# A fixed instruction order to the attention's end, and slot sums of several batches in TensorE column groups

## The chip, the core and the metric

One core of one Trainium2 chip runs the whole program. The metric is device microseconds of one execution, as the median of several runs. Engines are named as in the profile: PE (TensorE), ACT (ScalarE), DVE (VectorE), POOL (GpSimd), SP (SyncE, which issues nearly all DMAs).

## The reference, cut to what matters

Attention with a learned position bias, then a soft mixture of experts over all tokens, then a top-1 mixture.

```python
# attention: B, H, S, D = 4, 8, 576, 64
scores = q @ k.T / sqrt(D) + bias[h]            # bias: a small MLP of relative positions, 32 hidden
attn   = softmax(scores)                        # exp(s - max), divided by its sum
x      = attn @ v                               # -> [B*S, H*D] = [2304, 512]
# soft MoE: 8 experts, 4 slots each (32 slots), F = 1024
logits     = x @ phi                            # [2304, 32]
d          = exp(logits - logits.max(0)); d /= d.sum(0) + 1e-9      # over ALL 2304 tokens
slot_input = d.T @ x                            # [32, 512]: the slot sums
slot_out   = relu(slot_input[e] @ w1[e]) @ w2[e]                    # per expert, 4 slots each
c          = softmax(logits, over slots);  x = c @ slot_out
# then: skip gate, argmax expert, one dense expert per token, added to x
```

## The kernel before, in words

**Bias.** The position bias of all heads is built first by 36 calls of bias_batch and written to a DRAM scratch. The list order says in which sequence, and load_bias brings a head pair's rows back, 128 queries (t = 0 to 3; the last 64 of two heads are t = 4) at a time.

**Attention.** The work is 16 pairs n (head pair hp = n // 4, batch b = n % 4). ops_of(n) returns named steps of one pair. A name ends in p for the PE part and e for the evacuation: KG0p/KG0e, QG0p/QG0e, LASTp/LASTe are transposes of k and q and their copies; SW0, SW1, SW8 swap halves of k on POOL; QKtjp is the score product of query tile t, head j (line 412), QKtje its bias add with running minimum on DVE (line 429), EXtj the exponential on ACT (line 435). For t = 0 to 2, HIt (POOL, line 440) and LOt (DVE, line 444) split the result into two fp16 halves and TDt (line 449) is a transposing DMA issued on SP; for t = 3 and 4 PE transposes (T3ap to T3cp, T4ap, T4bp). AVtj are the products with v (lines 503 to 523), N0 and N1 the division into xnat (lines 544 to 556), XTp/XTe and XUp/XUe transposes of the result, LG0 and LG1 the logits of a pair's channels (lines 605 and 614), summed over hp in lgT. TD, LK, LQ, LV, BA, BM are SP's DMAs; BA of the last head pair loads expert weights (weight_piece) in place of bias.

**The order.** SCHED gives every step a number; todo sorts all steps of all pairs by n * II + number. Only the order counts, not the number's size. From the first score product up to 15 * II + first the steps are inside manual_schedule: each engine and SP run them exactly in that order. What lies behind that point (the last pair's later steps, the slot sums), the bias build and all that follows the attention are placed by the framework's planner, by its own cost estimate.

**Slot sums.** When the last head pair has its logits, for each batch: SA (slot_exp: maximum, negation, exponential with sum), SB (slot_T: five 32-wide transposes and a copy to dn), SC (slot_in: five fp32 products over token tiles, 32 output rows by 512 columns, lines 254 and 257, and two copies into sis). The four batches have different maxima, kept in nm; after the attention a matmul of nm with sel (line 744), a chain of small DVE/ACT steps (fx, fs, fz, lines 749 to 757) makes a factor for each batch and slot, and a product of sis with fsel (line 761) adds the four batches up. The result goes to sT, the stationary operand of the first expert product ph (line 773).

**Weights.** Both expert matrices are 64 pieces of 512 KB (weight_piece), i = 0 to 31 for w1 (line 773) and 32 to 63 for w2 (line 854). They rotate through 25 buffers: pieces 0 to 2 by BA; 3 to 12 in buffers of q, k and bias that are free late in the attention (NW + 10 = 13); 13 to 24 in twelve tiles x0 to x11 that lie where the attention's pools were. From piece 25 on, a piece is issued when the product that read its buffer is done. All go through SP's queue.

Of the kernel before, what the change touches and what calls it, by code (L numbers as in the profile page):

```python
# [59 lines left out]
def soft_moe_attention_kernel(ctx, tc, q, k, v, w1, b1, w2, phi, mw1, mw2,  # L60
# [168 lines left out]
    def slot_exp(b):  # L229
# [8 lines left out]
        act.activation(dT[r, 0:S], lgT[r, 0:S], AF.Exp, bias=nm[r, b:b + 1], scale=1.0, accum_out=nm[r, 4 + b:5 + b])  # L238

    def slot_T(b):  # L240

        r = slice(b * 32, (b + 1) * 32)
        pt = ps_t.tile([P, 512], F32, name="pt")
        dT = sl[0]
        for c in range(5):
            o = c * P if c < 4 or b % 2 == 0 else S - P
            pe.transpose(pt[:, c * NSL:(c + 1) * NSL], dT[r, o:o + P], ident[r, r])
        vec.tensor_copy(dn[:, b], pt[:, 0:5 * NSL])

# [1004 lines left out]
```

## Time and profile before

| | |
|---|---|
| median of 3 runs | 524.05 us (522.62 to 531.67) |
| profiled execution, its own time | 519.99 us |
| span from first to last instruction | 518.1 us |
| mean granted PE clock, share of 2.4 GHz | 0.942 |
| PE busy, of the span | 89% |
| DVE, ACT, POOL busy | 66%, 57%, 48% |
| last attention product ends | 346.6 us |
| first expert product begins | 391.7 us |
| last weights landed, second expert product ends | 450.6 us, 453.0 us |

The profiled execution is one run; times in the rows are microseconds from its first instruction. Its own time lies 4.06 us under the median of the timed runs, so a change in the span is carried over to the median as a difference.

### The profile page before, as it was taken

What the parts mean: (1) busy time and instruction counts of PE and PEld (TensorE: products, weight loads), DVE (VectorE), ACT (ScalarE), POOL (GpSimd) and SP (SyncE); (2) the same over time, 40 slices, a digit from 0 to 9 for tenths busy, and PEclk for the clock granted to TensorE, in tenths of its full rate; (3) what the DMA queues carried; (4) which work ended last, traced back from release to release, by engine and by line L of the source; (5) the groups of instructions that cost most, each with busy time, mean ns of one, the idle gap of its engine ahead of it and who ended that gap; (6) DMA issues with size and microseconds to landing.
All of it is one profiled execution on the core that took longest, in us unless ns stands there. A gap on an engine that the chain in (4) does not pass through costs nothing.

```text
span 518.1 us, 12026 instructions
## 1 busy us (share of the span) xinstructions
PE 460.6 (89%) x4539; PEld 347.0 (67%) x4539; DVE 344.0 (66%) x842; ACT 293.0 (57%) x565; POOL 247.2 (48%) x291
## 2 busy tenths in 40 slices
PE   4999989999999999999999999789759549769993
PEld 2566668999999899999999998662115224155472
DVE  6999966888887887778878786821231390046564
ACT  4889877877787787777887777411110021016610
POOL 5600049999889799797997994400020000001000
PEclk9999997999999999999999999988887958968999
DMA  6677658999999999999999999999003999845056
GB/s 175 222 258 259 213 198 189 219 206 224 198 229 192 220 216 220 214 211 210 185 203 211 231 221 214 269 320 373 1 1 120 394 387 387 296 143 183 22 173 202
DMA packets 154080, 111.53 MB, mean 215 GB/s; under 512 B 120257, under 2 KB 126913, under 8 KB 154017
## 3 DMA queue, kind: packets, MB, share of 16 engines
q1 hardware_dynamic: 152112, 107.47, 81.9%
q10 hardware_dynamic: 1824, 2.97, 1.7%
q8 instruction: 38, 0.62, 0.5%
q0 software_dynamic: 80, 0.26, 0.2%
q14 instruction: 26, 0.20, 0.1%
HBM read 66.97 MB, written 15.34 MB: 159 GB/s over the span
## 4 chain that ended last, share of the span: by engine, by line
PE 73%; DMA 11%; DVE 9%; issue 2%; POOL 2%; ACT 1%; SPq 0%; ACTq 0%; DVEq 0%; POOLq 0%
PE sc L412 14%; PE sc L155 10%; PE av L523 6%; PE av L507 5%; PE av L512 4%; DMA bias<-in_moe_w_dram 4%; PE pt L254 4%; PE pt L369 4%; PE pt L478 3%; DMA eT<-ehl 3%; PE pt L605 2%; DMA x<-in_moe_w_dram 2%; PE sc L418 2%; PE av L519 2%; PE ph L773 1%
## 5 line engine op out<-in xcount | busy, mean ns | idle before, releaser
L429 DVE CUSTOM_DVE_ANT_0 e<-sc,bias 128x576 f32<-128x576 f32 x128 | 95.2, 754 | 22.8 <-PE sc L412 22.4
L412 PE MATMUL sc<-k,qT 128*128 128x288 f32 x512 | 98.8, 321 | 1.7 <-POOL k L382 1.0
L435 ACT ACTIVATE e<-e,st 128x576 f32<-128x576 f32 x128 | 93.9, 771 | 5.2 <-DVE st L429 4.7
L440 POOL TENSOR_SCALAR ehl<-e 128x1152 f16<-128x1152 f32 x48 | 64.9, 1354 | 57.7 <-ACT e L435 56.0
L382 POOL TENSOR_SCALAR k<-k 64x512 fp32r<-64x512 f32 (+1 forms) x96 | 78.8, 821 | 20.5 <-ACT k L376 10.3
L412 PEld LDWEIGHTS sc<-k,qT 128*128 128x128 f32 x512 | 74.6, 195 | 7.5 <-DVE xnat L556 2.3
L444 DVE SCALAR_TENSOR_TENSOR ehl<-e,ehl 128x1152 f16<-128x1152 f32 x48 | 77.6, 1618 | 1.5 <-POOL ehl L440 1.5
L155 PE MATMUL sc<-hid,w2b 128*32 128x288 f32 x576 | 57.2, 420 | 3.0 <-DVE hid L151 3.0
L151 DVE TENSOR_SCALAR hid<-ll,nib 128x576 f32<-128x576 f32 x117 | 58.1, 574 | 0.0
L523 PE MATMUL av<-v,eT 128*128 128x65 f16 x1152 | 51.5, 194 | 0.0
L155 PEld LDWEIGHTS sc<-hid,w2b 128*32 128x32 f32 x576 | 32.3, 110 | 24.8 <-DVE hid L151 4.7
L523 PEld LDWEIGHTS <-eT 128*128 128x128 f16 x1152 | 44.4, 98 | 4.3 <-issue 3.3
L484 ACT ACTIVATE eTf<-pt 128x512 f32<-128x512 f32 (+1 forms) x48 | 23.5, 489 | 27.3 <-PE pt L478 27.2
L158 ACT ACTIVATE ev<-sc,offs,ipi 128x576 f32<-128x576 f32 x36 | 29.8, 828 | 10.4 <-PE sc L155 9.9
L981 POOL TENSOR_SCALAR Lt<-rk 128x128 f16<-128x128 f32 x1 | 0.3, 298 | 73.4 <-PE pbig L854 73.4
L507 PE MATMUL av<-tv,eTf 128*128 128x128 f32 x256 | 35.3, 280 | 0.0
L507 PEld LDWEIGHTS av<-tv,eTf 128*128 128x128 f32 x256 | 32.0, 191 | 0.0
L376 ACT ACTIVATE qT<-pt 128x512 fp32r<-128x512 f32 x32 | 19.1, 596 | 14.0 <-PE pt L369 13.8
L478 PE MATMUL pt<-ident,e 128*128 128x128 f32 x144 | 24.6, 282 | 0.9 <-ACT eTm L469 0.9
L327 POOL TENSOR_TENSOR sq<-tq,sq 128x576 fp32r<-128x576 f32 x16 | 23.1, 1441 | 1.3
L544 DVE TENSOR_SCALAR rs<-av 128x2 f32<-128x2 f32 (+1 forms) x64 | 8.0, 156 | 23.6 <-PE av L507 23.0
L327 POOL TENSOR_TENSOR sk<-tk,sk 128x576 fp32r<-128x576 f32 x16 | 23.0, 1435 | 1.3
(322 smaller groups left out, 871.6 us busy)
## 6 DMA issues: line engine op xcount, KB each, us to landing
x<-in_moe_w_dram SPq DMA_DIRECT2D x30, 512.0 KB, 10.6
scratch<-ev SPq DMA_DIRECT2D x36, 288.0 KB, 4.1
bias<-scratch SPq DMA_DIRECT2D x16, 576.0 KB, 4.9
tn<-in_v_dram SPq DMA_DIRECT2D x32, 224.0 KB, 4.9
bias<-in_moe_w_dram SPq DMA_DIRECT2D x13, 512.0 KB, 10.8
k<-in_moe_w_dram SPq DMA_DIRECT2D x12, 512.0 KB, 7.6
tk<-in_k_dram SPq DMA_DIRECT2D x16, 288.0 KB, 5.3
tq<-in_q_dram SPq DMA_DIRECT2D x16, 288.0 KB, 3.6
```

Source lines behind the costliest of these rows:

```text
L151: vec.tensor_scalar(out=hid, in0=src, scalar1=nib[:, gi:gi + 1], scalar2=None, op0=ALU.max)
L155: pe.matmul(pb[c * 32:(c + 1) * 32, hh, 0:288], lhsT=w2b, rhs=hid[:, hh * 288:(hh + 1) * 288], start=True, stop=True)
L327: pool.tensor_tensor(out=z[name][:, :, 1, :], in0=t, in1=z[name][:, :, 0, :], op=ALU.subtract)
L382: pool.tensor_scalar(out=k1[64 * i:64 * i + 64, :, u], in0=k0[64 - 64 * i:128 - 64 * i, :, u], scalar1=1.0, scalar2=1.0, op0=ALU.mult, op1 ...
L412: pe.matmul(sc[:, hh, 0:288], lhsT=l_, rhs=kf[i][:, o:o + 288], start=(i == 0), stop=(i == 1))
L429: vec.tensor_tensor_reduce(out=z["e", t][:, o].rearrange("p (a j) -> p a j", a=2), in0=z.pop(("sc", t, j))[:, :, 0:288], in1=bias_t[hp, t] ...
L435: act.activation(ee, ee, AF.Exp, bias=z["m", t][:, j:j + 1], scale=-1.0)
L440: pool.tensor_scalar(out=eh[:, 0], in0=z["e", t], scalar1=ES, scalar2=1.0, op0=ALU.mult, op1=ALU.mult)
L444: vec.scalar_tensor_tensor(out=eh[:, 1], in0=z.pop(("e", t)), scalar=ES, in1=eh[:, 0], op0=ALU.mult, op1=ALU.subtract)
L478: pe.transpose(pt[:, c], z["e", 3][:, (4 * g + c) * P:(4 * g + c + 1) * P], ident)
L507: pe.matmul(av[:, oj:oj + P], lhsT=eT[:, 5 * j + c], rhs=w, start=False, stop=j == 1 and c == 3)
L523: pe.matmul(av[:, oj:oj + VD], lhsT=eT[:, ei, 5 * j + c], rhs=v16[:, vi, c, j], start=False, stop=lastt and j == 1 and k_ == 2 and c == 3)
```

## The change: what it does

SCHED gets new numbers. The last four pairs (n = 12 to 15) get numbers of their own from a table LAST, one per pair, and manual_schedule now holds from the first score product to the last slot step. The bias batches are built in another sequence, with query tile t = 2 first. The weight pieces 3 to 12 are all issued behind the last transposing DMA of pair 15.

The slot steps become separate: SAm (maximum), SAx (exponential), SBp, SBe (transposes, copy), SC0 to SC4 (token tile c of batches 0, 1 and 2, each batch in its own group of 32 columns, into one PSUM tile), SCe and SCd (copies). Batch 3 is summed by S3p: its token tiles 0 to 3 go to the four column groups and tile 4 to group 0 again; the four partial rows stay apart in sis3, a borrowed e buffer, and are added up by the product FSp, which now has two operands (sl[1] and sis3) and so twice the matmuls. FX holds the factor chain of before, with four more copies on ACT for batch 3's factors; its tiles move to the const pool.

```diff
 II = 14100
-SCHED = {"LK": 0, "LQ": 607, "LV": 13878, "BA": 24197, "TD0": 34151, "TD1": 42871, "TD2": 32292, "KHI": 4505,
...
-         "LG0p": 64050, "LG0e": 65023, "LG1p": 73289, "LG1e": 73968}
+SCHED = {"LK": 0, "LQ": 2593, "LV": 9168, "BA": 20815, "BM": 30422, "TD0": 32207, "TD1": 41463, "TD2": 29378,
...
+         "EX31": 30379, "QK40p": 23432, "QK40e": 25178, "EX40": 26731, "HI0": 24394, "LO0": 26955, "AV00": 43025,
+         "AV01": 43844, "HI1": 30962, "LO1": 36034, "AV10": 43513, "AV11": 45277, "HI2": 23540, "LO2": 24437,
+         "AV20": 31523, "AV21": 33272, "T3ap": 30786, "T3ae": 31293, "T3bp": 32041, "T3be": 33438, "T3cp": 33299,
...
+         "XUp": 48366, "XUe": 49339, "LG0p": 56034, "LG0e": 56061, "LG1p": 57644, "LG1e": 58386}
+LAST = {"LK": [-1201, -2566, -6806, 1324], "LQ": [-3383, -757, -6246, 7269], "LV": [16548, 16126, 21689, 34057],
+         "BA": [25594, 164680, 55239, 158463], "TD0": [35809, 49689, 53834, 128993],
+         "TD1": [49729, 57859, 94140, 180561], "TD2": [35969, 41139, 51880, 83599], "KHI": [3363, -299, -219, 4361],
...
+         "QK11p": [21994, 21949, 43799, 92252], "QK11e": [22394, 27941, 51840, 108240],
...
+         "LG1e": [27941, 166501, 213593, 299837], "SAm0": [313897, 180561, 243397, 370297],
+         "SAx0": [160837, 205052, 257577, 376364], "SBp0": [418704, 271637, 290100, 382907],
+         "SBe0": [29484, 304160, 304160, 384437], "SAm1": 171293, "SAx1": 186623, "SBp1": 271597, "SBe1": 279301,
+         "SC0": 313937, "SC1": 325351, "SC2": 342097, "SC3": 397007, "SC4": 411147, "SCe": 481607, "SCd": 481727,
+         "FXp": 384397, "FX": 397047, "S3p": 404644, "S3e": 411107, "S3d": 481687, "FSp": 747365, "FSe": 767415}
...
+    fx = const.tile([NSL, 4], F32, name="fx")
+    fs = const.tile([NSL, 4], F32, name="fs")
+    fz = const.tile([NSL, 2], F32, name="fz")
+    fsel = const.tile([P, 2, NSL], F32, name="fsel")
+    fsx = const.tile([P, P], F32, name="fsx")
...
-    def slot_exp(b):
+    def slot_max(b):
...
-        dT = sl[0]
+            pool.memset(sl[1][96:P], 0.0)
         vec.tensor_reduce(out=nm[r, b:b + 1], in_=lgT[r, 0:S], axis=AX.X, op=ALU.max)
         vec.tensor_scalar(out=nm[r, b:b + 1], in0=nm[r, b:b + 1], scalar1=-1.0, scalar2=None, op0=ALU.mult)
-        act.activation(dT[r, 0:S], lgT[r, 0:S], AF.Exp, bias=nm[r, b:b + 1], scale=1.0, accum_out=nm[r, 4 + b:5 + b])
+
+    def slot_exp(b):
+        act.activation(sl[0][r, 0:S], lgT[r, 0:S], AF.Exp, bias=nm[r, b:b + 1], scale=1.0, accum_out=nm[r, 4 + b:5 + b])
...
     def slot_T(b):
-
         r = slice(b * 32, (b + 1) * 32)
-        pt = ps_t.tile([P, 512], F32, name="pt")
-        dT = sl[0]
+        pt = sl_pt[b] = ps_t.tile([P, 512], F32, name="pt")
         for c in range(5):
             o = c * P if c < 4 or b % 2 == 0 else S - P
-            pe.transpose(pt[:, c * NSL:(c + 1) * NSL], dT[r, o:o + P], ident[r, r])
-        vec.tensor_copy(dn[:, b], pt[:, 0:5 * NSL])
-
-    def slot_in(b):
-        r = slice(b * 32, (b + 1) * 32)
-        pt = ps_t.tile([P, 512], F32, name="pt")
-        for c in range(4):
-            pe.matmul(pt[r], lhsT=dn[:, b, c * NSL:(c + 1) * NSL], rhs=X[0][:, 4 * b + c, :], start=(c == 0), stop=False)
-        sis = sl[1]
-        u = slice((b % 2) * 64, (b % 2) * 64 + 64)
-        pe.matmul(pt[r], lhsT=dn[u, b, 4 * NSL:], rhs=X[0][u, 16 + b // 2, :], start=False, stop=True)
-        act.copy(sis[r, 0:256], pt[r, 0:256])
-        vec.tensor_copy(sis[r, 256:512], pt[r, 256:512])
+            pe.transpose(pt[:, c * NSL:(c + 1) * NSL], sl[0][r, o:o + P], ident[r, r])
+
+    def slot_dn(b):
+        vec.tensor_copy(dn[:, b], sl_pt.pop(b)[:, 0:5 * NSL])
+
+    def slot_sum(b, c, dst, start, stop):
+        u = slice((b % 2) * 64, (b % 2) * 64 + 64) if c == 4 else slice(0, P)
+        pe.matmul(dst, lhsT=dn[u, b, c * NSL:(c + 1) * NSL], rhs=X[0][u, 4 * b + c if c < 4 else 16 + b // 2, :], start=start, stop=stop)
+
+    sl_pt = {}
 
...
         if hp == 3 and b:
             for i, bb in enumerate(bs):
-                for x, f in (("SA", slot_exp), ("SB", slot_T), ("SC", slot_in)):
+                for x, f in (("SAm", slot_max), ("SAx", slot_exp), ("SBp", slot_T), ("SBe", slot_dn)):
                     ops[f"{x}{i}"] = lambda f=f, bb=bb: f(bb)
+        if n < NP - 1:
+            return ops
+
+        def sc(c):
+            if c == 0:
+                z["sl"] = ps_s.tile([P, 2, 512], F32, name="sc")
+            for bb in range(3):
+                slot_sum(bb, c, z["sl"][bb * 32:(bb + 1) * 32, 0], c == 0, c == 4)
+
+        each([f"SC{c}" for c in range(5)], sc)
+
+        @part
+        def SCe():
+            act.copy(sl[1][0:96, 0:256], z["sl"][0:96, 0, 0:256])
+
+        @part
+        def SCd():
+            vec.tensor_copy(sl[1][0:96, 256:512], z["sl"][0:96, 0, 256:512])
+
+        @part
+        def FXp():
+            z["pf"] = ps_t.tile([P, 512], F32, name="pt")
+            pe.matmul(z["pf"][0:NSL, 0:8], lhsT=sel[:, 0:NSL], rhs=nm, start=True, stop=True)
+
+        @part
+        def FX():
+            pf = z["pf"]
+            vec.tensor_reduce(out=fz[:, 0:1], in_=pf[0:NSL, 0:4], axis=AX.X, op=ALU.min)
+            act.activation(fx, pf[0:NSL, 0:4], AF.Exp, bias=fz[:, 0:1], scale=-1.0)
+            vec.tensor_tensor(out=fs, in0=fx, in1=pf[0:NSL, 4:8], op=ALU.mult)
+            vec.tensor_reduce(out=fz[:, 1:2], in_=fs, axis=AX.X, op=ALU.add)
+            vec.tensor_scalar(out=fz[:, 1:2], in0=fz[:, 1:2], scalar1=1e-9, scalar2=None, op0=ALU.add)
+            vec.reciprocal(out=fz[:, 1:2], in_=fz[:, 1:2])
+            vec.tensor_scalar(out=fx, in0=fx, scalar1=fz[:, 1:2], scalar2=None, op0=ALU.mult)
+            for g in range(4):
+                act.activation(fsel[g * 32:(g + 1) * 32, 1], sel[0:NSL, 0:NSL], AF.Copy, scale=fx[:, 3:4])
+                if g < 3:
+                    vec.tensor_scalar(out=fsel[g * 32:(g + 1) * 32, 0], in0=sel[0:NSL, 0:NSL], scalar1=fx[:, g:g + 1],
+                                      scalar2=None, op0=ALU.mult)
+
+        @part
+        def S3p():
+            z["s3"] = ps_s.tile([P, 2, 512], F32, name="sc")
+            for c in range(5):
+                g = c % 4 * 32
+                slot_sum(3, c, z["s3"][g:g + 32, 0], c < 4, c in (1, 2, 3, 4))
+            z["sis3"] = e_p.tile([P, 2 * S], F32, name="e")[:, 0:512]
+
+        @part
+        def S3e():
+            act.copy(z["sis3"][:, 0:256], z["s3"][:, 0, 0:256])
+
+        @part
+        def S3d():
+            vec.tensor_copy(z["sis3"][:, 256:512], z["s3"][:, 0, 256:512])
+
+        @part
+        def FSp():
+            z["pfs"] = ps_t.tile([P, 512], F32, name="pt")
+            for kc in range(4):
+                for i, x in enumerate((sl[1], z["sis3"])):
+                    pe.matmul(z["pfs"][:, kc * NSL:(kc + 1) * NSL], lhsT=x[:, kc * P:(kc + 1) * P], rhs=fsel[:, i],
+                              start=i == 0, stop=i == 1)
+
+        @part
+        def FSe():
+            vec.tensor_copy(fsx, z["pfs"][:, 0:P])
+
...
-    for i, x in enumerate(("SA0", "SA1", "SB0", "SB1", "SC0", "SC1")):
-        SC[x] = SC["LG1e"] + 1000 + 500 * i
-    SC["BM"] = 35452
-    todo = sorted((n * II + SC[x], n, x) for n in range(NP) for x in OPS[n])
+    SC["BM"] = 30422
+
+    def place(n, x):
+        if n < NP - 4:
+            return SC[x]
+        return LAST[x][n - NP + 4] if type(LAST[x]) is list else LAST[x]
+
+    todo = sorted((n * II + place(n, x), n, x) for n in range(NP) for x in OPS[n])
...
-    order = [*range(8), *range(16, 24), *range(8, 16), *range(32, 36), *range(24, 32)]
+    order = [*range(16, 24), *range(16), *range(24, 36)]
...
-    msc = None
-    for t_, n, x in todo:
-        on = first + 0 <= t_ < 15 * II + first + 0
-        if on and not msc and 'PE Pool Activation DVE SP':
-            msc = ExitStack()
-            msc.enter_context(tc.manual_schedule(engines={getattr(mybir.EngineType, x) for x in 'PE Pool Activation DVE SP'.split()}))
-        elif not on and msc:
-            msc.close()
-            msc = None
-        if True:
+    with tc.manual_schedule(engines=fixed):
+        last_td = max(place(NP - 1, f"TD{t}") for t in range(3)) + (NP - 1) * II
+        for t_, n, x in todo:
             OPS[n][x]()
-            if n == NP - 1 and x in {'TD0': 1, 'TD1': 1, 'TD2': 2}:
-                for _ in range({'TD0': 1, 'TD1': 1, 'TD2': 2}[x]):
+            if t_ == last_td:
+                while len(wq) < NW + 10:
                     weight_piece()
-    if msc:
-        msc.close()
-    while len(wq) < NW + 10:
-        weight_piece()
...
-        pf = p1.tile([P, 10], F32, name="pw")
-        pe.matmul(pf[0:NSL, 0:8], lhsT=sel[:, 0:NSL], rhs=nm, start=True, stop=True)
...
-        for b in range(4):
-            vec.tensor_scalar(out=fsel[b * 32:(b + 1) * 32], in0=sel[0:NSL, 0:NSL], scalar1=fx[:, b:b + 1],
-                              scalar2=None, op0=ALU.mult)
-        pt = ps.tile([P, 512], F32, name="pc")
-        for kc in range(4):
-            pe.matmul(pt[:, kc * NSL:(kc + 1) * NSL], lhsT=sis[:, kc * P:(kc + 1) * P], rhs=fsel, start=True, stop=True)
-
...
-            pt[:, 0:P].rearrange("p (k e i) -> p e k i", k=4, e=E))
+            fsx.rearrange("p (k e i) -> p e k i", k=4, e=E))
```

Sorted by their numbers, PE's last steps after the change are: QK11p.15 T4bp.15 T3ap.15 AV20.15 T3bp.15 AV40.15 XUp.14 AV41.15 AV21.15 LG1p.13 XTp.14 AV30.15 T3cp.15 LG0p.14 AV31.15 AV00.15 LG1p.14 AV10.15 AV01.15 AV11.15 XUp.15 SBp1.13 SBp0.13 XTp.15 SBp0.14 LG0p.15 LG1p.15 SC0 SC1 SC2 SBp0.15 FXp SC3 S3p SC4 FSp (the number behind the point is the pair). SP's last are: TD2.14 TD0.14 BA.14 TD1.14 TD2.15 TD0.15 BA.13 BA.15 TD1.15, then pieces 3 to 12.

## Rows read from the trace of the kernel before

**Rows 1.** Windows, of three pair periods: length, each engine's busy time, granted clock, DMA share, GB/s

```profile
69.75:86.56 16.81, 14.03 (x84) 12.40 (x83) 11.65 (x28) 13.47 (x26) 13.89 (x15) 0.80 0.75 181
...
288.35:305.16 16.81, 16.81 (x202) 15.55 (x202) 13.12 (x36) 14.13 (x29) 16.00 (x17) 1.00 1.12 227
...
321.98:338.79 16.81, 13.98 (x156) 11.69 (x154) 11.13 (x28) 7.83 (x15) 5.68 (x25) 0.98 1.08 270
```

**Rows 2.** Chain that ended last, 346 to 392 us: start, length, what

```profile
346.27 0.32 PE av L507 x2
...
350.66 0.42 DVE xnat L556
...
351.93 5.23 PE pt L254 x8
357.16 0.97 PE pt L257 x2
358.14 3.55 PE pt L254 x8
...
363.56 0.66 PE pt L581 x4
...
379.58 5.10 PE pt L254 x8
...
386.54 0.16 DVE fz L749
...
389.16 1.66 PE pc L761 x8
...
391.73 6.92 PE ph L773 x85
```

**Rows 3.** Windows, of the stretches around the slot sums

```profile
365.00:392.00 27.00, 17.61 (x52) 5.95 (x56) 6.93 (x23) 2.95 (x8) 3.22 (x3) 0.83 0.02 1
```

**Rows 4.** Chain that ended last, 408 to 453 us: the two expert products

```profile
408.65 0.64 PE ph L773 x8
...
427.36 2.14 PE pbig L854 x8
...
439.84 10.71 DMA x<-in_moe_w_dram
450.59 2.36 PE pbig L854 x8
```

**Rows 5.** Windows, while the weights stream and from logits to transposed exponentials

```profile
374.40:379.60 5.20, 1.81 (x11) 0.63 (x10) 2.58 (x6) 1.47 (x4) 3.22 (x3) 0.96 0.00 0
...
440.00:450.00 10.00, 7.93 (x32) 1.01 (x28) 0.00 (x0) 0.00 (x0) 0.00 (x0) 1.00 1.03 381
```

**Rows 6.** Timeline of SP, DMA issues around the attention's end

```profile
322.51 3.77 SPq L186 DMA_DIRECT2D bias<-in_moe_w_dram  x3
...
327.72 12.47 SPq L449 DMA_TRANSPOSE eT<-ehl  x3
```

**Rows 7.** Chain that ended last, 254 to 272.5 us: first and last of 49 pieces

```profile
253.95 0.13 PE sc L418
...
272.13 0.44 PE pt L478 x4
```

**Rows 8.** Page, groups by line: busy us, mean ns of one, idle before

```profile
L429 DVE CUSTOM_DVE_ANT_0 e<-sc,bias 128x576 f32<-128x576 f32 x128 | 95.2, 754 | 22.8 <-PE sc L412 22.4
...
L435 ACT ACTIVATE e<-e,st 128x576 f32<-128x576 f32 x128 | 93.9, 771 | 5.2 <-DVE st L429 4.7
L440 POOL TENSOR_SCALAR ehl<-e 128x1152 f16<-128x1152 f32 x48 | 64.9, 1354 | 57.7 <-ACT e L435 56.0
...
L444 DVE SCALAR_TENSOR_TENSOR ehl<-e,ehl 128x1152 f16<-128x1152 f32 x48 | 77.6, 1618 | 1.5 <-POOL ehl L440 1.5
```

**Rows 9.** Tile ehl, 200 to 340 us: its transposes from issue to landing

```profile
DMA to landing us min/median/max: 4.6/6.6/8.9
```

**Rows 10.** Timeline of PE, one product over four column groups

```profile
479.20 1.07 PE L1082 MATMUL y<-w2e,hO 128*32 128x512 f32 x8
```

More of the change, by code (lines that the diff above doesn't have):

```diff
@@ L35 @@
 II = 14100
-SCHED = {"LK": 0, "LQ": 607, "LV": 13878, "BA": 24197, "TD0": 34151, "TD1": 42871, "TD2": 32292, "KHI": 4505,
[12 rows of a table removed]
+SCHED = {"LK": 0, "LQ": 2593, "LV": 9168, "BA": 20815, "BM": 30422, "TD0": 32207, "TD1": 41463, "TD2": 29378,
+         "KHI": 5296, "KLO": 7286, "QHI": 7955, "QLO": 8985, "VA": 16708, "VH": 23835, "VLO": 29151, "KG0p": 8978,
[11 rows of a table added]
+LAST = {"LK": [-1201, -2566, -6806, 1324], "LQ": [-3383, -757, -6246, 7269], "LV": [16548, 16126, 21689, 34057],
+         "BA": [25594, 164680, 55239, 158463], "TD0": [35809, 49689, 53834, 128993],
+         "TD1": [49729, 57859, 94140, 180561], "TD2": [35969, 41139, 51880, 83599], "KHI": [3363, -299, -219, 4361],
+         "KLO": [6397, 1171, 4429, 7389], "QHI": [4641, 6462, 7409, 15359], "QLO": [5278, 6502, 7729, 15439],
[35 rows of a table added]
+         "XTe": [96094, 111599, 152361, 283051], "XUp": [332440, 78392, 134552, 213593],
[7 rows of a table added]
 ETB = 4
@@ L65, in soft_moe_attention_kernel @@
     const = ctx.enter_context(tc.tile_pool(name="const", bufs=1))
+    fixed = {getattr(mybir.EngineType, x) for x in ('PE', 'Activation', 'DVE', 'Pool', 'SP')}
     dpool = ctx.enter_context(tc.tile_pool(name="dpool", bufs=1, space=DRAM))
@@ L74, in soft_moe_attention_kernel @@
     identr = const.tile([P, P], F32R, name="identr")
+    fx = const.tile([NSL, 4], F32, name="fx")
[3 more added lines that the diff above has]
+    fsx = const.tile([P, P], F32, name="fsx")
     scratch = dpool.tile([S, H, S], F32, name="scratch")
     pool.memset(nm, 0.0)
+    pool.memset(fsel, 0.0)
     kctx = ctx.enter_context(ExitStack())
@@ L237, in slot_exp @@
         vec.tensor_scalar(out=nm[r, b:b + 1], in0=nm[r, b:b + 1], scalar1=-1.0, scalar2=None, op0=ALU.mult)
-        act.activation(dT[r, 0:S], lgT[r, 0:S], AF.Exp, bias=nm[r, b:b + 1], scale=1.0, accum_out=nm[r, 4 + b:5 + b])
+    def slot_exp(b):
+        r = slice(b * 32, (b + 1) * 32)
+        act.activation(sl[0][r, 0:S], lgT[r, 0:S], AF.Exp, bias=nm[r, b:b + 1], scale=1.0, accum_out=nm[r, 4 + b:5 + b])
     def slot_T(b):
         r = slice(b * 32, (b + 1) * 32)
-        pt = ps_t.tile([P, 512], F32, name="pt")
-        dT = sl[0]
+        pt = sl_pt[b] = ps_t.tile([P, 512], F32, name="pt")
         for c in range(5):
             o = c * P if c < 4 or b % 2 == 0 else S - P
-            pe.transpose(pt[:, c * NSL:(c + 1) * NSL], dT[r, o:o + P], ident[r, r])
-        vec.tensor_copy(dn[:, b], pt[:, 0:5 * NSL])
-    def slot_in(b):
-        r = slice(b * 32, (b + 1) * 32)
-        pt = ps_t.tile([P, 512], F32, name="pt")
-        for c in range(4):
-            pe.matmul(pt[r], lhsT=dn[:, b, c * NSL:(c + 1) * NSL], rhs=X[0][:, 4 * b + c, :], start=(c == 0), stop=False)
-        sis = sl[1]
-        u = slice((b % 2) * 64, (b % 2) * 64 + 64)
-        pe.matmul(pt[r], lhsT=dn[u, b, 4 * NSL:], rhs=X[0][u, 16 + b // 2, :], start=False, stop=True)
-        act.copy(sis[r, 0:256], pt[r, 0:256])
-        vec.tensor_copy(sis[r, 256:512], pt[r, 256:512])
+            pe.transpose(pt[:, c * NSL:(c + 1) * NSL], sl[0][r, o:o + P], ident[r, r])
[5 more added lines that the diff above has]
+    sl_pt = {}
     def ops_of(n):
@@ L741, in soft_moe_attention_kernel @@
         pool.memset(hT, 0.0)
-        pf = p1.tile([P, 10], F32, name="pw")
-        pe.matmul(pf[0:NSL, 0:8], lhsT=sel[:, 0:NSL], rhs=nm, start=True, stop=True)
-        fx = sp.tile([NSL, 4], F32, name="fx")
-        fs = sp.tile([NSL, 4], F32, name="fs")
-        fz = sp.tile([NSL, 2], F32, name="fz")
-        fsel = sp.tile([P, NSL], F32, name="fsel")
-        vec.tensor_reduce(out=fz[:, 0:1], in_=pf[0:NSL, 0:4], axis=AX.X, op=ALU.min)
-        act.activation(fx, pf[0:NSL, 0:4], AF.Exp, bias=fz[:, 0:1], scale=-1.0)
-        vec.tensor_tensor(out=fs, in0=fx, in1=pf[0:NSL, 4:8], op=ALU.mult)
-        vec.tensor_reduce(out=fz[:, 1:2], in_=fs, axis=AX.X, op=ALU.add)
-        vec.tensor_scalar(out=fz[:, 1:2], in0=fz[:, 1:2], scalar1=1e-9, scalar2=None, op0=ALU.add)
-        vec.reciprocal(out=fz[:, 1:2], in_=fz[:, 1:2])
-        vec.tensor_scalar(out=fx, in0=fx, scalar1=fz[:, 1:2], scalar2=None, op0=ALU.mult)
-        for b in range(4):
-            vec.tensor_scalar(out=fsel[b * 32:(b + 1) * 32], in0=sel[0:NSL, 0:NSL], scalar1=fx[:, b:b + 1],
-                              scalar2=None, op0=ALU.mult)
-        pt = ps.tile([P, 512], F32, name="pc")
-        for kc in range(4):
-            pe.matmul(pt[:, kc * NSL:(kc + 1) * NSL], lhsT=sis[:, kc * P:(kc + 1) * P], rhs=fsel, start=True, stop=True)
         vec.tensor_copy(
             sT.rearrange("p (e x) -> p e x", x=132)[:, :, 0:128].rearrange("p e (k s) -> p e k s", s=NSL)[:, :, :, 0:4],
-            pt[:, 0:P].rearrange("p (k e i) -> p e k i", k=4, e=E))
+            fsx.rearrange("p (k e i) -> p e k i", k=4, e=E))
         ph = p1.tile([P, 256], F32, name="ph")
@@ L872, in soft_moe_attention_kernel @@
         ctl = ExitStack()
-        fixed = {getattr(mybir.EngineType, x) for x in ('PE', 'Activation', 'DVE', 'Pool', 'SP')}
         ctl.enter_context(tc.manual_schedule(engines=fixed))
```

54 rows, old and new, of tables (LAST, SCHED) are left out of this document.

## The prediction

> **What bounds the kernel now.** I read four views in this order. First the windows cut at the pair period of the repeating part [rows 1]: from 288.35 to 305.16 us PE is busy for all 16.81 us, at full clock, while DVE has 3.7 us to spare. So the attention costs what PE has to do. The first period (14.03 us busy, clock 0.80) and the last (13.98 us) are the ones with holes. Then the chain of work that ended last [rows 2]. The attention's last product ends at 346.59; the first expert product begins at 391.73. In these 45.1 us PE does the slot sums one batch after the other: 6.20 us (5.23 + 0.97), 4.54, 6.3 and 6.1, and between them waits for small steps. The reader should see that 32-column products stand there alone. Third, what the DMAs do meanwhile [rows 3]: from 365 to 392 us their share is 0.02. All 25 weight buffers are full and nothing is freed before the first expert product reads them. Fourth, the chain behind 392 us [rows 4]: it runs through weight DMAs until 450.55, where PE has 2.36 us left to do. From 391.73 to 450.55 the kernel waits for 39 pieces of 512 KB. At the 381 GB/s of that stretch [rows 5] a piece takes 1.376 us, and 39 take 53.7; the other 5.1 us are the start. So time before the first expert product delays the stream, and the stream sets the end: what is removed there comes off the total one for one until the DMAs have no idle time left.
>
> **Part one: the order up to the last score product.** SCHED's new order changes no PE work, so I cost the repeating part at nothing: the cover is PE's own 16.81 us per period. If the cover is gone (PE waits for something in each period), it costs 15 times the wait; that is the rival below. The head can gain or lose some of the 2.8 us PE idle in the first period plus its lower clock: I take 0, bounds -3 and +3.
>
> **Part two: the last pairs.** SP before issues three weight pieces by 326.3 ahead of the last three transposes, which then take 12.47 us to issue, 4.2 each [rows 6]; the other weights follow them from 340 on. After the change pieces 3 to 12 stand behind TD1 of pair 15, and only two pieces (BA.13, BA.15; 3.77 / 3 = 1.3 us each) stand before it. From the 49 pieces of PE's chain in the steady part [rows 7] I add up what PE has still to do at 305.16: 35.0 us to the end of the attention, so 340.2 without idle time, and 340.8 with pair 14's logits, which the new order puts before the end. Of this 9.2 us lie behind QK11p of pair 15, which so ends at 331.6. Behind it a chain must run: about 0.7 us until DVE has done N0.14, then QK11e 0.84 (0.754 and the accumulator), EX11 0.77, HI1 1.35, LO1 1.62 [rows 8], with handovers 5.5: LO1 is done at 337.1. SP is free for TD1 between 337.1 (nothing queued) and 341.4 (TD0 4.2 behind LO0, then two weight pieces 2.5); I take 340, nearer to the queued end, since all three issues are in the new order. The transpose lands 4.6 to 8.9 us after issue, median 6.6 [rows 9]; AV10, AV01 and AV11 take 1.3. The attention then ends at 340 + 6.6 + 1.3 = 348, bounds 343 and 351.6. That is no gain over 346.6: the new order has less waiting for late transposes, but it does pair 14's logits earlier and its last chain is 16 us long where PE has only 9.2 us to fill it. TD1 is issued by 344.
>
> **Part three: from the last product to the expert product.** Removed: four single sums, 23.1 us of PE. Added: five steps SC0 to SC4 for three batches at once, and S3p. The trace has the same shape elsewhere: eight 512-column passes over four column groups take 1.07 us [rows 10], against 8 x 0.44 = 3.55 us in one group at full clock [rows 2]. I take 1.07 for a step, and twice that as the other bound, since passes of 0.44 us took about 0.87 in the stretches of these sums at the lower clock (5.23 us for the same eight). The chain: N0 0.8; XTp 0.66; its copy 0.6 (an estimate from the 0.77 of 576 columns); logits, maximum, exponential, transposes and copy to dn 5.2, the whole stretch 374.40 to 379.60 of before, which has just these steps. In it PE must also do SC0 to SC2, 3.2 us, in the 1.85 us in which SAm and SAx run: 1.35 more (4.5 at the lower clock). Then SC3, of which 0.34 lies beside the copy: 0.73; S3p, two steps, 2.04; SC4 0.97; copies 0.43 (an estimate from the 0.42 us of the DVE pass of that width that N0 ends with); FSp 3.32, as its 16 passes are twice the 1.66 of before; FSe and the copy to sT 0.6. The sum is 16.7 us, with handovers 17; all steps at the lower clock make 23.6, none of them visible 14.5. FX (386.54 to 389.16, 2.6 us, and some 0.9 for four more ACT copies) is costed at nothing: S3p and SC4 cover it with 3.0 us on PE, and S3e waits behind it on ACT for 0.5 at most; without the cover it costs 3.5. Batches 0 to 2 no longer stand in the path; what is late next is batch 3's own logits. The expert product so begins at 365, 26.7 us earlier; FSp ends at 364.4.
>
> **Part four: the weights.** Two limits. (a) SP starts the 61 pieces behind TD1 at 344: 344 + 2.5 (half of the 5.1 us start above; bounds 0 and 5.1) + 61 x 1.376 = 430.4. (b) sis3 borrows an e buffer, over which x tiles are laid later. By the tile sizes in the code it lies under x5 or a later x tile, so SP, in order, can stand at piece 18 until FSp has read sis3: 364.4 + 2.5 + 46 x 1.376 = 430.2. Both give 430. The gap of [rows 3] is gone, but the stream itself now is the limit: of 26.7 us gained at the expert product 20.3 come through. Behind the stream nothing changes: hidden behind it, the 18.1 us from the first expert product's end (409.29) to the second's start (427.36, [rows 4]) still fit: the last w1 piece lands near 386, so the second can start near 405, and it caught up with the stream in 12.5 us (427.36 to 439.84), which is before 430.
>
> **The sum.** The stream ends 20.3 us earlier, 430.2 for 450.55. The profiled execution goes from 519.99 to 499.7. The median of the runs shown is 4.06 above it; carried over as a difference, 524.05 - 20.3 = 503.7.
>
> **The rivals.** *PE waits for the transposes in every period (slower side).* In the new order AV20 of a pair stands between QK21p and QK01p of the next. From it PE has 5.6 us to QK30p; then QK30e 0.84, LO2 1.62, TD2 to landing. With 6.6 us this closes in 14.7, below 16.81. It decides from the point where issue wait and landing exceed 8.7: the longest landing seen is 8.9, and if TD2 also stands behind TD1 of the pair before (4.2 here) it is 6.6 + 4.2 = 10.8, so 2.1 us per period, 15 periods, 32 us: 503.7 + 32 = 535. For it: DMA share 1.12 in the steady window. Against it: LO1 of the earlier pair ends well before LO2 in DVE's new order, so TD1 should be out by then. *The shapes are changed too often.* PE goes between 128-row, 64-row and transpose shapes six times in this tail. The two 64-row passes took 0.97 us where two others at full clock take 0.89, so some 0.1 per change is what the trace shows. If each change instead waited out a pass of 0.44 to 0.87, or the groups ran one after the other in S3p and SC3, 3 to 8 us more: 507 to 512. The Trainium skill ("TensorEngine Tiling (Array Packing)", Key Properties) says that changing the tiling mode, not merely the tile, drains TensorE, which speaks against this order; the same section says that different tiles run in parallel. The 1.07 us agree with the second, the 0.97 us show only little of the first. *The last pair's chain is longer*, as in-order engines wait on each other where the planner could step aside, or each period loses 0.3 to 0.6 us: 509 to 516. *More is gained:* head and last pairs leave PE no idle time and TD1 lands early, the attention ends at 343 and the stream starts at 338: 492 to 498.
>
> **How the numbers follow.** The forecast, 498 to 509 with its likeliest at 503.7, has 0.66; more gained 0.12; shapes 0.08; longer chain 0.08; waits in every period 0.06. The range from 494 to 513 leaves out half of the first rival, the upper part of the third and a little at the low end. A change of 2% is 513.6, about what a measurement of this kernel can tell from none. Faster by over 2%: 0.89 (0.78, 0.07 and 0.04); within: 0.07; slower: 0.04.
>
> **What would show it.** Right: pair windows still 16.81 with PE full; the L412 products end near 332; slot sums as two short groups, 5 us between LG and dn; the expert product near 365; DMA share near 1 without a gap from 344 to 430; from there 69 us as before. Wrong: PE idle before AV in the repeating windows (first rival); sums of 3 us a step (second); a DMA gap between 350 and 370 (SP standing at an x tile, earlier than I think); or the planner, which places what follows FSp, putting other work before the expert product.

## The result and the profile after

The changed kernel has a median of 504.23 us (500.30 to 509.63, four runs), the kernel before 523.34 in the same comparison. The ratio is 0.964, 95% interval 0.956 to 0.972: faster by 3.6%, some 19 us. The forecast was 503.7, range 494 to 513. The profiled execution took 505.48 us, its span 503.7, against 519.99 and 518.1 before. Executions here come in a faster and a slower state; each ratio compares the faster ones with those of the kernel before on the same chip, while medians are of all.

First the windows of the same three pair periods as in [rows 1], and two others, as "length, busy time of PE, PEld, DVE, ACT, POOL, then granted clock, DMA share, GB/s":

```profile
69.75:86.56 16.81, 13.72 (x129) 12.01 (x128) 13.92 (x28) 14.08 (x29) 13.62 (x15) 1.00 0.69 164
204.27:221.09 16.82, 15.77 (x196) 15.02 (x195) 12.35 (x35) 12.99 (x27) 14.57 (x15) 1.00 1.20 231
254.72:271.53 16.81, 15.67 (x180) 14.12 (x179) 11.09 (x31) 10.65 (x22) 14.93 (x15) 1.00 0.93 212
288.35:305.16 16.81, 15.56 (x180) 13.62 (x180) 12.83 (x23) 11.88 (x25) 13.57 (x15) 1.00 0.56 124
321.98:338.79 16.81, 14.41 (x165) 12.87 (x162) 9.64 (x33) 9.05 (x18) 3.84 (x4) 0.90 0.61 126
```

PE is no longer full everywhere: the window that had 16.81 us of PE work has 15.56. The other windows between 86 and 254 us still show 16.4 to 16.8. Pair 12, the first that LAST places, begins its score products at 262.06 us, so the windows behind 254.72 hold the last pairs more than the repeating part. What PE waited for is in the view of waits from 86 to 356 us (us in total, times, longest):

```profile
PE av L571 <- DMA eT<-ehl: 9.5, 5, 5.4
PE sc L464 <- POOL k L434: 1.5, 2, 1.1
PE sc L464 <- DVE st L481: 0.9, 1, 0.9
```

Three of them as they stand in PE's timeline, at AV20 of pair 8, at the first score product of pair 12 and at one of pair 14:

```profile
217.09 0.34 PE L571 MATMUL av<-vt,eT 128*128 128x130 f16 x3 [1.05 <-DMA eT<-ehl]
...
263.87 0.40 PE L464 MATMUL sc<-k,qT 128*128 128x288 f32 x1 [1.14 <-POOL k L434]
...
303.02 1.21 PE L464 MATMUL sc<-k,qT 128*128 128x288 f32 x6 [0.89 <-DVE st L481]
```

The waits for transposes are the first rival in small: three times up to 322 us the transpose comes after PE is ready for AV20 (1.05 us in pair 8, 0.2 in pair 12, 0.4 in pair 14), and then for 2.4 us at AV00 of pair 14 and 5.4 us at AV10 of pair 15. Next SP's timeline at the attention's end, which answers to [rows 6]:

```profile
325.50 18.29 SPq L501 DMA_TRANSPOSE eT<-ehl  x3
343.84 1.06 SPq L240 DMA_DIRECT2D w<-in_moe_w_dram  x2
345.03 6.12 SPq L501 DMA_TRANSPOSE eT<-ehl  x1
351.19 0.58 SPq L240 DMA_DIRECT2D sq<-in_moe_w_dram  x1
```

The last transpose (TD1 of pair 15) is issued at 345.03 and holds SP for 6.12 us; the 61 weight pieces begin at 351.19. Now PE's timeline from the attention's end to the expert product, the stretch of [rows 2]:

```profile
355.70 0.37 PE L646 MATMUL pt<-ident,xnat 64*128 64x64 f32 x1
...
359.35 1.07 PE L309 MATMUL sc<-xnat,dn 128*32 128x512 f32 x3
...
360.91 1.89 PE L309 MATMUL sc<-xnat,dn 128*32 128x512 f32 x12
363.38 0.49 PE L302 MATMUL pt<-ident,bias 32*128 32x32 f32 x5 [0.59 <-ACT bias L295]
...
363.89 2.88 PE L309 MATMUL sc<-xnat,dn 128*32 128x512 f32 x20
367.67 0.38 PE L740 MATMUL pt<-fsel,bias 128*128 128x32 f32 x2 [0.90 <-ACT bias L692]
...
370.32 0.64 PE L866 MATMUL ph<-bias,sT 128*32 128x256 f32 x8
```

The attention ends at 355.8. 14.5 us later the first expert product begins; before, it took 45.1. The slot sums (L309) are two short groups, one beside batch 3's own small steps and one of 2.88 us. The weights meanwhile (windows; [rows 3] and [rows 5] are their counterparts), and the last piece in the chain that ended last:

```profile
365.00:392.00 27.00, 22.05 (x294) 10.93 (x287) 17.61 (x37) 5.84 (x16) 0.00 (x0) 1.00 1.03 398
400.00:435.80 35.80, 27.76 (x106) 3.74 (x104) 0.00 (x0) 0.00 (x0) 0.00 (x0) 1.00 1.03 378
```

```profile
435.87 2.36 PE pbig L947 x8
```

The gap in the DMA is gone (share 1.03 and 398 GB/s where it was 0.02 and 1), and the stream ends at 435.87 for 450.59. Behind it 67.8 us are left of the span, 67.5 before. So what the profile gained, 14.4 us of span, all lies ahead of the stream's end.

Six of the profiles below (one group, one group with its own place, ten weights early, and the three that follow from it with sis3 in its own place) are of executions whose whole attention was some 6 to 11 us late from a stall in the head, which is shown in the last section; of these only distances from a common event are compared.

### The profile page after: what moved, and what is told of

It reads as the page before. It is cut to its first block, busy times and chain, and to the rows that moved or that the text cites. A ratio compares the mean times of both kernels' runs of the same rounds, so it can differ in the third digit from the quotient of the medians.

```text
span 503.7 us, 12027 instructions
## 1 busy us (share of the span) xinstructions
PE 449.4 (89%) x4547; PEld 337.8 (67%) x4547; DVE 340.8 (68%) x840; ACT 292.8 (58%) x567; POOL 247.8 (49%) x293
## 4 chain that ended last, share of the span: by engine, by line
PE 58%; DMA 23%; DVE 7%; POOL 4%; issue 3%; SPq 2%; ACT 1%; DVEq 0%; POOLq 0%; ACTq 0%
PE sc L464 11%; PE sc L209 10%; DMA x<-in_moe_w_dram 8%; DMA bias<-in_moe_w_dram 6%; PE av L575 5%; PE av L559 5%; PE av L564 4%; DMA eT<-ehl 4%; PE pt L421 3%; PE pt L530 2%; POOL k L434 2%; DMA rk<-in_c_rk_dram 2%; PE pt L657 2%; PE sc L470 2%; DVE ehl L496 1%
## 5 line engine op out<-in xcount | busy, mean ns | idle before, releaser
L492 POOL TENSOR_SCALAR ehl<-e 128x1152 f16<-128x1152 f32 x48 | 63.4, 1322 | 74.8 <-ACT e L487 66.1
L434 POOL TENSOR_SCALAR k<-k 64x512 fp32r<-64x512 f32 (+1 forms) x96 | 77.1, 803 | 12.2 <-ACT k L428 5.5
L464 PEld LDWEIGHTS sc<-k,qT 128*128 128x128 f32 x512 | 73.0, 191 | 12.0 <-POOL k L434 4.1
L496 DVE SCALAR_TENSOR_TENSOR ehl<-e,ehl 128x1152 f16<-128x1152 f32 x48 | 74.1, 1544 | 2.7 <-POOL ehl L492 2.7
L947 PE MATMUL pbig<-x,hT 128*32 128x512 f32 x76 | 20.2, 605 | 5.4 <-DMA x<-in_moe_w_dram 5.4
L571 PE MATMUL av<-vt,eT 128*128 128x130 f16 x144 | 16.4, 223 | 9.5 <-DMA eT<-ehl 9.5
## 6 DMA issues: line engine op xcount, KB each, us to landing
bias<-in_moe_w_dram SPq DMA_DIRECT2D x13, 512.0 KB, 10.2
k<-in_moe_w_dram SPq DMA_DIRECT2D x12, 512.0 KB, 10.2
```

The source lines that it names most:

```text
L434: pool.tensor_scalar(out=k1[64 * i:64 * i + 64, :, u], in0=k0[64 - 64 * i:128 - 64 * i, :, u], scalar1=1.0, scalar2=1.0, op0=ALU.mult, op1 ...
L464: pe.matmul(sc[:, hh, 0:288], lhsT=l_, rhs=kf[i][:, o:o + 288], start=(i == 0), stop=(i == 1))
L492: pool.tensor_scalar(out=eh[:, 0], in0=z["e", t], scalar1=ES, scalar2=1.0, op0=ALU.mult, op1=ALU.mult)
L496: vec.scalar_tensor_tensor(out=eh[:, 1], in0=z.pop(("e", t)), scalar=ES, in1=eh[:, 0], op0=ALU.mult, op1=ALU.subtract)
```

## The experiments

Two distances order them all: from the issue of the first weight behind the last transpose ("start") to the last pass of the second expert product, and from the first pass of the first expert product (ph) to the same.

| kernel | start | ph | last pass | from start | from ph |
|---|---|---|---|---|---|
| before | - | 391.73 | 450.59 | - | 58.9 |
| after | 351.19 | 370.32 | 435.87 | 84.7 | 65.6 |
| after, again (first) | 347.99 | 369.55 | 433.05 | 85.1 | 63.5 |
| after, again (second) | 349.72 | 370.33 | 435.00 | 85.3 | 64.7 |
| first weights early | 343.73 | 365.59 | 428.82 | 85.1 | 63.2 |
| transposes later | 345.60 | 366.31 | 430.87 | 85.3 | 64.6 |
| one group | 359.36 | 393.32 | 452.43 | 93.1 | 59.1 |
| one group, own place | 359.40 | 391.84 | 450.04 | 90.6 | 58.2 |
| before with groups | - | 381.55 | 440.82 | - | 59.3 |

With 61 pieces the last pass stands 85 us behind the start (61 x 1.376 = 83.9, and 1.2), or 58 to 59 behind ph, whichever is later. The second number is the 39 pieces that need a freed buffer, 53.7 us, about 4 until the first such piece goes out, and about 1 behind the last. So in the changed kernel the start binds, with 4 to 7 us to spare at ph.

**The change again**, as the yardstick of the first chip. No edit.

> The changed kernel once more, as the yardstick of this group of runs. Theory (the stream of weights behind the last transpose sets the end): ratio to the kernel before 0.962 to 0.970, weights without a gap from about 351 to 436 us, the last ones landed about 84 us after the last transpose is issued. Rival (the first expert product's start sets the end): the DMAs pause between 350 and 375 us.

Ratio 0.9641 [0.9592, 0.9691], median 503.67. Its last transpose went out at 343.20 and the stream began at 347.99: of one kernel, this start scatters by 3 us between executions.

**One column group.** The order stays; all four sums lie in one column group, each in a PSUM bank of its own:

```
-                slot_sum(bb, c, z["sl"][bb * 32:(bb + 1) * 32, 0], c == 0, c == 4)
+                slot_sum(bb, c, z["one"][bb], c == 0, c == 4)
...
-                g = c % 4 * 32
-                slot_sum(3, c, z["s3"][g:g + 32, 0], c < 4, c in (1, 2, 3, 4))
+                slot_sum(3, c, z["one"][3], c == 0, c == 4)
```

> The changed order, with all four slot sums in one column group (every product ends in PSUM rows 0 to 31 of its own bank), so that none runs beside another; the copies of three batches become three each. PE has 20 products of 0.87 us for 7 steps of about 1: some 10 us more before the first expert product, which moves from 370 to about 380. Theory (the stream sets the end, the product waits for it anyway): 0 to 4 us slower than the changed kernel. Rival (time before the expert product counts one for one): 9 to 12 us slower.

Ratio 0.9826 [0.9755, 0.9897], so the groups are worth some 9.7 us of the 18.7. (The edit also copies the three batches one by one, which is part of this: from the last sum to the final product the chain has 2.8 us for 0.9.) The chain shows the sums:

```profile
370.21 8.90 PE sc L309 x17
...
379.69 7.88 PE sc L309 x20
```

Passes that the changed kernel runs 20 in 2.88 us take 7.88 for 20 in one group. The expert product comes 38.9 us behind the last transpose's issue for 26.4, 12.5 later, and the last pass 98.0 for 89.9, 8.2 later. SP's waits show one place where it stood, the x tile over sis3's borrowed e buffer (piece 23, counted from 0), which the prediction had as limit (b):

```profile
SPq L240 <- DVE e L736: 8.3, 1, 8.3
...
SPq L240 <- PE pt L743: 3.0, 1, 3.0
```

That the stream would hide the sums was wrong. Whether this stand or the late expert product did it was tested next.

**One column group, sis3 in a place of its own.** As the last, and `z["sis3"] = sl[0][:, 0:512]` for the e buffer.

> All four sums in one column group as before, so the first expert product is some 12 us later, but sis3 lies in sl[0]. In the run with one group the last w2 pass came 98.0 us after the issue of the last transpose, against 89.9 with groups, and SP stood 8.3 us at an x tile over sis3. Theory, this stand carried the loss: then only the buffers that the first expert product frees are late, 38.9 + 1 + 39 x 1.376 = 93.6 us after the last transpose, a ratio to before near 0.971. Rival, the later expert product itself carries it: 98 us again, ratio near 0.982.

Ratio 0.9815 [0.9733, 0.9897]: the same as with the borrowed buffer. The stand is gone, yet the last pass is 97.0 us behind the last transpose (98.0). SP's timeline and the chain:

```profile
395.47 0.34 SPq L240 DMA_DIRECT2D sq<-in_moe_w_dram  x1
```

```profile
391.84 7.68 PE ph L869 x105
...
450.04 2.36 PE pbig L950 x8
```

The 26th piece goes out 3.6 us behind ph, 39 x 1.376 follow: 391.84 + 3.6 + 53.7 = 449.1. The rival holds: the late expert product carries the loss, and the theory had erred by taking 1 us for these 3.6.

**Groups alone, in the order before.** Batches 0 to 2 as one sum in three groups, batch 3 in four, and with that the final product over two operands as in the change; the order of the steps up to there stays:

```
+            for bb in range(3):
+                slot_sum(bb, c, pt[bb * 32:(bb + 1) * 32], c == 0, c == 4)
...
+            g = c % 4 * 32
+            slot_sum(3, c, pt[g:g + 32], c < 4, c in (1, 2, 3, 4))
```

> The kernel before with the column groups alone: batches 0 to 2 summed over three groups, batch 3 over four, two operands in the final product, nothing of the order changed. There the DMAs stand still for 27 us before the first expert product. Theory (what is taken from the path counts in full until the stream is the limit): the sums shrink from 23.1 to about 8 us of PE, of which some must still wait for batch 3; 10 to 16 us faster than the kernel before, ratio 0.970 to 0.981. Rival (the order alone makes the gain, the sums hide behind the stream): less than 4 us faster, ratio above 0.992.

Ratio 0.9822 [0.9751, 0.9893], just short of what was expected. Its chain answers to [rows 2] and [rows 4]:

```profile
357.67 6.71 PE pt L253 x30
...
369.78 3.79 PE pt L253 x10
...
381.55 6.22 PE ph L790 x77
...
440.82 2.36 PE pbig L871 x8
```

The expert product is 10.2 us earlier and the stream ends 9.8 earlier: in the order before, time at ph came through one for one. Each half of the change alone is worth some 9 us, both 19. What inside the order brings its half (the last pairs, the slot steps, the place of the weights, the sequence of the bias) was not tried apart.

**First weights early.** The pieces of pairs 13 to 15 that stand ahead of the last transposes go out before TD1 of pair 12:

```
-         "BA": [25594, 164680, 55239, 158463], ...
+         "BA": [25594, 35500, 21420, 7340], ...
```

> The changed kernel with one difference: the three weight pieces of the last head pair's BA steps are issued together ahead of TD1 of pair 12, at about 290 us, where the trace shows 6 us with hardly any DMA, and no longer between the last transposes. Theory (the last transpose stands behind 1 MB of weights, and the stream starts when it is issued): the last transpose is issued in 3 us for 6.1, its products start 3 us earlier, the stream starts near 347 for 351.2 and ends near 431.5 for 435.8: 4 us faster than the changed kernel. Rival (the expert product's start or PE's work sets the end): within 1 us of the changed kernel.

In the profile the stream starts at 343.73 for 347.99 and ends at 428.82 for 433.05, 4.2 us earlier, as expected:

```profile
341.28 2.40 SPq L501 DMA_TRANSPOSE eT<-ehl  x1
343.73 0.78 SPq L240 DMA_DIRECT2D sq<-in_moe_w_dram  x1
```

The last transpose holds SP for 2.4 us, for 4.75 in the change again, and the stream starts 3.0 us behind the end of LO1 for 6.4; the other 0.8 us are an earlier LO1. The timing doesn't show it: 0.9651 [0.9604, 0.9698], against 0.9641 for the change. A gain of some 4 us in one trace is no more than the executions scatter.

**Ten weights early.** On top of it four more pieces go behind TD0 of pair 14 and three behind TD2 of pair 15, so that 54 are left (the bias buffers that some of them take are used in the order 0, 2, 3, 1):

```
+            for _ in range({(NP - 2, "TD0"): 4, (NP - 1, "TD2"): 3}.get((n, x), 0)):
+                weight_piece()
```

> On top of the experiment with the first three weights early (stream start 343.7, last w2 pass at 428.8 in its profile) seven more 512 KB pieces are issued earlier, four behind TD0 of pair 14 and three behind TD2 of pair 15, so that 54 of the 64 are left behind the last transpose for 61. Theory A, the stream's start and length are the only limit: 7 x 1.376 = 9.6 us less, last pass near 419, median near 493. Theory B, SP in its order is the limit: it stands at the small load of the gate (w) until Pool has cleared the tile, and Pool clears it behind sT, which waits for the last logits on PE; in the profile with the first weights early this load went out at 359.1 and 49 pieces stood behind it: 359.6 + 1 + 49 x 1.376 = 428. Then nothing is gained, and DMA falls idle for some us before 360, as the queue has fewer pieces in it.

Ratio 0.9637 [0.9572, 0.9703], median 504.72: nothing gained, as theory B has it. SP's timeline:

```profile
362.19 0.37 SPq L240 DMA_DIRECT2D x<-in_moe_w_dram  x1
368.45 0.39 SPq L928 DMA_DIRECT2D w<-in_moe_w_gate_dram  x1
```

```profile
437.36 2.37 PE pbig L949 x8
```

SP stands for 5.9 us at the gate's small load. From the second of the two small loads, at 368.89, theory B's sum gives 368.9 + 1 + 49 x 1.376 = 437.3; measured 437.36.

**Gate early.** The same with w10 in the constants' pool and its two loads before the first pair.

```
+    w10 = const.tile([P, 4, 10], F32, name="w10")
...
+    sync.dma_start(out=w10[:, :, 0:8], in_=gate.rearrange("(k p) e -> p k e", p=P))
```

> As the one before, but the gate's small tile w10 has a place of its own and its loads go out before the first pair. If B held there, the stand at 359 is gone and the next limit decides. Either the x tile over sis3's borrowed e buffer, where SP can go on only when FSp has read it (about 365.5), with 41 pieces behind: 365.5 + 2.5 + 41 x 1.376 = 424; or that stand is covered by what is queued, and the last pass is near 419.5. Median 493 to 498. If A held there, no difference.

Median 498.45, ratio 0.9593 [0.9529, 0.9657]. The stand at the gate is gone and the next shows, at sis3's buffer, in SP's waits and the chain:

```profile
SPq L242 <- DVE e L735: 6.5, 1, 6.5
```

```profile
369.54 10.01 PE ph L872 x160
...
428.20 2.35 PE pbig L949 x8
```

The last pass is 58.7 us behind ph, as in the table, so ph binds. The stand is close behind it: piece 23 goes out at 368.61, and theory B's sum gives 368.6 + 1 + 41 x 1.376 = 426.0 for the measured 428.20.

**Gate early, sis3 in its own place**, run twice.

> As the one before, and sis3 lies in sl[0], which is free after the last transposes of the exponentials, instead of a borrowed e buffer. If the x tile's wait was the limit there, the last pass comes to 419.5 to 420.5 (25 buffers, the 26th piece waits for the first expert product near 366, 39 pieces behind it: 366 + 1 + 53.7), some 4 us less. If the stand was covered, no difference.

> Ten weights early, gate early, sis3 in its own place, once more, for a profile without the late attention that the first one had. Theory: the stand of 6.5 us at the x tile over sis3 (in the profile with the gate early) is gone and the first expert product is the limit: last w2 pass 57 to 58 us behind it, against 58.7 with the stand, and median 495 to 497. Rival: the stand was covered by what was queued; then both profiles agree and the median is 498.5.

Ratios 0.9534 [0.9459, 0.9609] and 0.9622 [0.9532, 0.9711], medians 498.66 and 501.54. The last pass is 57.1 and 57.8 us behind ph, against 58.7 with the stand. So the stand cost at most about 1 us in the trace and the rest of it was covered; the timings can't tell it from nothing. Both medians lie above what was expected, and both profiles have the late attention, so the expected end of the stream near 420 stays untested.

**The transposes' products later.** In the twelve pairs that SCHED places, AV20 moves behind QK01p of the next pair and T3bp on PE: `"AV20": 32100` for 31523. It ran against the change again, on the same chip.

> The changed kernel once more, as the yardstick of this chip for the three others: median 503 to 505, last w2 pass 433 to 436, which is 62 to 66 us behind the start of the first expert product.

> AV20 moved behind QK01p of the next pair and T3bp on PE, about one us later; nothing else is changed. Theory: PE's waits for the transposes at AV20 (2.2 and 1.7 us in all between 86 and 322 us in two profiles of the changed kernel) are part of why the attention ended later than forecast; they go to 0.3 or less, the last transpose and the stream start 1 to 2 us earlier, median 1 to 2 us under the yardstick. Rival: PE waits elsewhere for the same time, as the other holes (score products behind Pool's k and DVE's st) come from steps before it; then the waits go and the end of the attention stays.

The yardstick's median is 508.74, above what was expected, the edit's 510.94. Ratios 0.9688 [0.959, 0.9786] for the change and 0.9735 [0.9609, 0.986] for the edit, both wide: the timings show no gain. In the traces PE's waits for transposes between 86 and 322 us, the change first, then the edit:

```profile
PE av L571 <- DMA eT<-ehl: 0.9, 3, 0.5
```

```profile
PE av L571 <- DMA eT<-ehl: 0.2, 1, 0.2
```

This doesn't show the theory. None of the yardstick's 0.9 us stands at an AV20 that the edit moves: 0.46 are at AV10 of pair 9, 0.20 and 0.29 at AV20 of pairs 12 and 14, which LAST places. And first weights early, with AV20 in its old place, shows the same 0.2. The 1.05 us at pair 8 in the first profile of the change (1.72 in the second) come and go without an edit.

The edit's last transpose does go out at 340.67 (344.96 in the yardstick, 343.20 and 345.03 in the other two profiles of the change), and the last pass comes at 430.87 for 435.00. The largest part of this arises behind the moved steps. Windows of PE alone, the change first, then the edit:

```profile
322.00:338.80 16.80, 14.27 (x155) 0.90 0.60 124
```

```profile
322.00:338.80 16.80, 16.48 (x210) 1.00 0.57 120
```

In that window PE waits 2.5 us at AV00 of pair 14 in the yardstick and 0.3 with the edit. The transpose before that product took 6.3 us from issue to product for 4.7; in the other two profiles of the change it took 6.3 and 4.7 too. So this is scatter of the change itself, and whether AV20's place costs anything stays open.

**All of it**: ten weights, gate, own place, AV20.

> Ten weights early, gate early, sis3 in its own place, and AV20 moved as in the other run. Its last w2 pass is set by the first expert product, 57 to 59 us behind it (57.1 and 58.7 in the two earlier runs of this form); if AV20 gives 1 to 2 us there, the median is 494 to 495, otherwise 495 to 497.

Median 495.74, ratio 0.9516 [0.9444, 0.9588], last pass 56.8 us behind ph. It beats the kernel before by 4.8% and lies below the changed kernel of the same comparison (0.9688 [0.959, 0.9786]), the intervals just apart. Against the form without the AV20 edit (0.9622 [0.9532, 0.9711], same chip) they overlap, so nothing is shown for that edit here either.

## Why the prediction was right, step by step

**Part one, the repeating part at nothing: nearly right.** In the twelve pairs that SCHED places PE waits 1.4 us in the first profile of the change (0.3 for Pool's k, 1.05 for a transpose at AV20), 2.0 and 0.7 in the other two, and never over 0.15 at a time with first weights early. The first rival was right in mechanism and far too large in size: PE waits at AV20 in one of the twelve pairs in two of the three profiles, for 1.05 and 1.72 us, and in none in the third.

**Part two, the last pairs: right in the chain, 7 us too early.** The last score products end near 338.8 (forecast 331.6), LO1 at 343.4 (337.1), TD1 is issued at 345.0 (340) and holds SP for 6.1 us (4.2), the stream starts at 351.2 (344), the attention ends at 355.8 (348, bounds 343 and 351.6). The other two profiles of the change have 343.2 and 345.0 for TD1, 348.0 and 349.7 for the stream. The term that failed is PE's remaining work "without idle time". PE's waits from 86 us to the last score product are 7.0 us, nearly the whole miss at that point: the 1.4 above, about 3 in pairs 12 to 14 that recur in every profile (1.1 for Pool's k, 0.9 for DVE's st and smaller ones; why these come late was not tried), and 2.4 at AV00 of pair 14. The same sum holds elsewhere. In the change again (twice), first weights early and transposes later the waits are 5.5, 6.0, 4.7 and 3.2 us, so 331.6 becomes 337.1, 337.6, 336.3 and 334.8; measured are 337.0, 338.7, 336.2 and 334.5 (within 0.3 us, and 1.1 in the second repeat).

Behind LO1 the rest is SP and the two pieces ahead of TD1. With them TD1 goes out 1.6 us behind LO1 and holds SP for 4.7 to 6.1 us (four profiles); without them, in first weights early, ten weights early and gate early, 0.1 to 0.5 us behind it and for 2.4 to 2.8 us.

**Part three, to the expert product: 14.5 us for 17**, the lower bound. The step of column groups was rightly priced from [rows 10]: 20 passes took 2.88 us, 0.144 each, where 1.07 for eight is 0.134. SC0 to SC2 (1.35 in the sum) and FX cost nothing visible, and FSp's 16 passes took 1.9 us for 3.32. The second rival, that changing shapes or serial groups cost 3 to 8 us, is out. One group shows what serial passes would have cost: 12.5 us at ph, of which 1.9 are that edit's own copies.

**Part four, the stream: right.** Limit (a), from the measured start, gives 351.2 + 2.5 + 83.9 = 437.6, measured 435.9. Limit (b) didn't bind; it exists, but at piece 23 and not 18. What stands close behind (a) is another limit that the prediction had only for the kernel before: ph + 58, since 39 pieces wait for freed buffers. It is why one column group lost some 8 us in spite of the stream.

**The sum.** The stream was to end at 430.2 and ended at 435.9, so the profiled execution came to 505.5 for 499.7. That the median is within 0.6 us of the forecast is partly luck: the changed kernel's profiled execution stood 1.25 us above its median, the one before 4.06 below the median then shown, and the forecast carried the second difference over.

## What to carry to other kernels

Where a stream of loads sets the end, write its end as the later of several sums (from its first free issue, from the first buffer freed, from each wait in its queue's order) and see how close the second stands: it says how much of a gain comes through. Small loads in the same in-order queue count among them; one of 16 KB, waiting for a cleared tile, held up in the trace what seven early pieces of 512 KB should have brought. Products of few columns that stand alone on PE are worth spreading over column groups, but the gain is read at what waits for them.

## What the hardware showed that was not expected

In six of the fourteen profiles one Pool operation in the head, 64 x 512 of k, took 15.06 to 15.08 us instead of 0.6 to 0.8. The timeline of the second run with sis3 in its own place, Pool and then DVE:

```profile
16.29 15.08 POOL L436 TENSOR_SCALAR k<-k 64x512 fp32r<-64x512 f32 x1 [3.77 <-ACT k L430]
```

```profile
8.77 22.12 DVE L207 TENSOR_SCALAR hid<-ll,nib 128x576 f32<-128x576 f32 x45
...
18.78 12.10 DVE L207 TENSOR_SCALAR hid<-ll,nib 128x576 f32<-128x576 f32 x28
```

(The second row is a part of the first, from a narrower window.) In the change again, without the stall, DVE's row is:

```profile
9.18 27.17 DVE L205 TENSOR_SCALAR hid<-ll,nib 128x576 f32<-128x576 f32 x46
```

Pool's operation ends at 31.37, 0.48 us after DVE's 45 back-to-back operations end at 30.89. Behind it SP's next load of k goes out at 35.7, in the other profiles at 20.6 to 21.4; PE idles 11.8 us, and the attention is 6 to 11 us late to its end. The Trainium skill ("Trainium Architecture — The Big Picture", What this means for kernel authors) says that DVE and GpSimd share a port pair by an exclusive lock, not by splitting its bandwidth. The trace agrees with that, as Pool moved again only when DVE paused. In the profiles without the stall Pool's same operations took 0.62 to 0.79 us beside a DVE row without gaps too, but there DVE needed 0.59 us for each operation (27.17 us, 46) and not 0.43 (12.10 us, 28), so it looks as if the two took turns. What decides between the two was not tried.

The runs of one kernel differ by about such an amount. In the six profiles with the stall the profiled execution lies 1.4 to 8.8 us above the median of its kernel, in the other eight between 7.5 below and 1.3 above. So the stall goes with the longer executions; that it alone parts them is not shown.
